# Moving one 4-matmul transpose group behind the weights that were already there

## The chip, the cores and the metric

The kernel runs on one core of a Trainium2 chip. The metric is the device time of one execution in microseconds (us), lower is better. Each comparison is between runs on the same chip; between chips the kernel before moves by a few tenths of a microsecond.

## The reference, cut to what matters

```python
kv  = einsum('bhsd,bhse->bhde', k, v)            # linear attention, batch 8, 8 heads, 576 rows, 64 wide
out = einsum('bhsd,bhde->bhse', q, kv)
out = out / sqrt(mean(out*out, -1) + 1e-6) * g_norm
x   = out as [8, 576, 512]
xn  = (x - mean) / sqrt(var + 1e-6) * g_ln
y   = x + maximum(xn @ w1, 0) @ w2               # w1 is 512 x 2048, w2 is 2048 x 512
```

The rows are cut into 36 tiles of 128. Four tiles come from batch 0's first 512 rows; each needs one "slot" of q. w1 and w2 are loaded in four quarters each.

## The kernel before: the parts that matter

All loads of q, k, v and the weights are issued by GpSimd into one queue, in the order of these lines (each load casts float32 to bfloat16; an extract):

```python
    pool_load(("q", 0, 1), load_slot(qp[0], q, 0, 1), rate1)
    load_w(0, 1)
    pool_load(("q", 0, 2), load_slot(qp[0], q, 0, 2), rate1)
    load_w(1, 1)                                            # w1, second quarter
    load_w(2, 1)                                            # w1, third quarter
    pool_load(("q", 0, 3), load_slot(qp[0], q, 0, 3), rate1)  # last q slot
    load_w(3, 1)                                            # w1, fourth quarter
    ...   # w2's first quarter, batch 1's k and v, w2's second quarter, batch 1's q, the rest of w2
```

A q slot is turned by four TensorE transposes into PSUM, and one copy (by ScalarE or VectorE) takes the result to SBUF. Then four "out" matmuls use it:

```python
    def add_q_turn_pe(b, t, deps, key, eng, h0=0, h1=H):
        ...
        s = add("PE", 0.24 * w, 0.24 * w + 0.26, key, [ident] + list(deps), ..., alloc=("mm", "kvt")[b])
        ...
        e = add(eng, occ, dur, key, [s], lambda: q_turn_out(...))
        s.frees = e
```

The first layer for the first eight tiles works in groups of 16 matmuls, one tile by one quarter of w1 (`m1_fine`):

```python
            g = add("PE", 0.89, 1.1, i, done[a]["xT"] + load["w", 1, c], lambda: m1_fine(a, c), alloc="mm", main=True)
```

Nothing runs in the order of these lines. Each `add` makes a step with a key, and a planner (`run_plan`), with its own estimates of durations, picks the order of every engine before the program is built. On the chip each engine keeps that order. So a changed key can move other steps too, and the order of the built program has to be looked at.

## Time and profile before

| | before |
|---|---|
| time, median of the first three runs | 293.84 us (293.79 to 294.05) |
| profiled span | 292.0 us |
| TensorE busy | 283.9 us, 97% |
| VectorE / ScalarE / GpSimd busy | 57% / 49% / 22% |

### The profile page before, as it was taken

To read this page: it belongs to the slowest core of one execution; us is meant where nothing else is said; L and a number is where in the kernel's file an instruction comes from. 1 tells how busy PE (TensorE), PEld (TensorE's weight loads), DVE (VectorE), ACT (ScalarE), POOL (GpSimd) and SP (SyncE) were. 2 spreads that over 40 slices of the span, in tenths; PEclk is the share of its full clock that TensorE was granted. 3 is DMA by queue.
4 is the path that set the end of the run, shared out by engine and by line. 5 is a ranking of instruction groups with operands and counts; after the bars stand their busy time and mean duration, and the time that the engine had idled before them with its cause. 6 is when DMAs were issued, how large, how long until landed. Compare 5 with 4: busy or idle time off the path is not lost.

```text
span 292.0 us, 5183 instructions
## 1 busy us (share of the span) xinstructions
PE 283.9 (97%) x2057; PEld 161.1 (55%) x2057; DVE 165.2 (57%) x361; ACT 142.6 (49%) x288; POOL 65.6 (22%) x93
## 2 busy tenths in 40 slices
PE   8879999999999999999999999999999999999995
PEld 6668955977745445444544445444544444444444
DVE  2695049578974997557655775477557755320022
ACT  2377964787856612761276127612761177017400
POOL 8974220006407205404050406000000000000000
PEclk9999999999999999999999999999999999999999
DMA  6999999965999997994999399912201310120012
GB/s 98 185 199 205 203 199 170 250 77 76 177 201 111 164 153 161 171 178 105 203 91 174 81 188 119 187 55 90 56 18 54 92 54 18 56 90 18 0 74 73
DMA packets 108716, 35.60 MB, mean 122 GB/s; under 512 B 87187, under 2 KB 104467, under 8 KB 108692
## 3 DMA queue, kind: packets, MB, share of 16 engines
q0 software_dynamic: 72624, 18.35, 65.8%
q1 hardware_dynamic: 35828, 16.79, 26.8%
q8 instruction: 16, 0.26, 0.4%
q10 hardware_dynamic: 240, 0.13, 0.2%
q14 instruction: 8, 0.07, 0.1%
HBM read 36.70 MB, written 9.44 MB: 158 GB/s over the span
## 4 chain that ended last, share of the span: by engine, by line
PE 91%; DMA 4%; POOL 3%; issue 0%; DVE 0%; POOLq 0%
PE mm_ps L643 43%; PE mm_ps L624 33%; PE mm_ps L609 9%; DMA qp<-in_q_dram 4%; PE out_ps L478 3%; PE kv_ps L455 3%; POOL qp L267 1%; PE xT_ps L559 1%; POOL w L348 1%; POOL vb L246 1%; POOL kb L246 1%; PE qT_ps L414 0%; POOL identity masks.py:197 0%; DVE x L650 0%; POOL identity masks.py:199 0%
## 5 line engine op out<-in xcount | busy, mean ns | idle before, releaser
L643 PE MATMUL mm_ps<-w,m 128*128 128x512 bf16 (+2 forms) x608 | 129.5, 368 | 0.0
L624 PE MATMUL mm_ps<-xT,w 128*128 128x512 bf16 x448 | 100.6, 379 | 0.0
L631 ACT ACTIVATE m<-mm_ps 128x512 bf16<-128x512 f32 x112 | 66.8, 597 | 51.4 <-PE mm_ps L624 50.6
L643 PEld LDWEIGHTS <-m 128*128 128x128 bf16 x608 | 57.3, 98 | 60.8
L624 PEld LDWEIGHTS <-w 128*128 128x128 bf16 x448 | 43.1, 98 | 48.9
L500 DVE TENSOR_REDUCE ss<-sq 128x8 f32<-128x512 f32 (+1 forms) x37 | 24.8, 669 | 48.4 <-ACT sq L491 48.4
L650 DVE SCALAR_TENSOR_TENSOR x<-mm_ps,rstd,x 128x512 f32<-128x512 f32 (+2 forms) x38 | 27.2, 719 | 41.7 <-PE mm_ps L643 41.7
L491 ACT ACTIVATE sq<-out_ps 128x512 f32<-128x512 f32 (+1 forms) x37 | 21.5, 584 | 44.4 <-PE out_ps L478 44.4
L609 PE MATMUL mm_ps<-xT,w 128*128 128x128 bf16 x512 | 30.6, 219 | 0.1
L609 PEld LDWEIGHTS <-w 128*128 128x128 bf16 x512 | 29.2, 98 | 1.2 <-issue 0.2
L552 DVE SCALAR_TENSOR_TENSOR xc<-x,mv,gl 128x512 bf16<-128x512 f32 (+1 forms) x38 | 27.2, 723 | 1.1
L495 DVE TENSOR_TENSOR xg<-out_ps,gn 128x512 f32<-128x512 f32 (+1 forms) x37 | 24.7, 668 | 0.2
L616 ACT ACTIVATE m<-mm_ps 128x512 bf16<-128x512 f32 x32 | 18.7, 598 | 5.7 <-PE mm_ps L609 5.5
L728 POOL COPY mark<-xT 128x1 bf16<-128x1 bf16 x15 | 6.5, 435 | 57.4 <-DMA xT<-xc 53.4
L530 DVE TENSOR_TENSOR x<-xg,inv 128x512 f32<-128x512 f32 x24 | 16.6, 692 | 0.8
L504 ACT ACTIVATE rms<-ss,eps_attn 128x8 f32<-128x8 f32 (+1 forms) x37 | 11.1, 300 | 12.1 <-DVE ss L500 11.9
L546 DVE BATCH_NORM_STATS2 stats<-x 128x6 f32<-128x512 f32 x24 | 16.6, 690 | 0.5
L478 PEld LDWEIGHTS <-qT 128*128 128x128 bf16 x160 | 11.3, 98 | 7.1 <-ACT qT L394 1.0
L478 PE MATMUL out_ps<-kv_pack,qT 128*128 128x128 bf16 x160 | 14.5, 219 | 0.6 <-ACT qT L394 0.6
L466 DVE CAST kv_pack<-kv_ps 64x256 bf16<-64x256 f32 x14 | 5.9, 422 | 12.9 <-PE kv_ps L455 12.8
L455 PEld LDWEIGHTS <-kp 128*128 128x128 bf16 (+1 forms) x168 | 10.4, 99 | 2.6 <-DVE kp L396 0.5
L274 POOL DMA_DIRECT2D qp<-in_q_dram x5 | 11.4, 2287 | 0.9 <-issue 0.9
(64 smaller groups left out, 177.3 us busy)
## 6 DMA issues: line engine op xcount, KB each, us to landing
out_dram<-x SPq DMA_DIRECT2D x30, 256.0 KB, 3.2
w<-in_moe_w_ch_dram POOLq DMA_DIRECT2D x8, 512.0 KB, 12.4
vb<-in_v_dram POOLq DMA_DIRECT2D x6, 512.0 KB, 11.6
kp<-in_k_dram POOLq DMA_DIRECT2D x5, 512.0 KB, 8.7
qp<-in_q_dram POOLq DMA_DIRECT2D x5, 512.0 KB, 10.3
out_dram<-x SPq DMA_DIRECT2D x10, 128.0 KB, 3.0
qb<-in_q_dram POOLq DMA_DIRECT2D x2, 512.0 KB, 18.0
qp<-in_q_dram POOLq DMA_DIRECT2D x10, 64.0 KB, 9.9
```

The lines of the kernel that those rows point to most:

```text
L455: nc.tensor.matmul(ps[:, hp, :], lhsT=kp[b % 2][p, t, 2 * hp:2 * hp + 2, :].rearrange("p h d -> p (h d)"), rhs=(v5[b % 2][:, 2 * hp:2 * hp ...
L478: nc.tensor.matmul(o3[:, hp, :], lhsT=att[b]["qT"][:, 4 * t + hp, :], rhs=kv_pack[b % 3][:, hp, :], start=(i == 0), stop=(i == len(bs) - 1))
L491: nc.scalar.activation(sq[:, h0:h1, :], st[n]["ps", h0][:, h0:h1, :], func=AF.Square)
L495: nc.vector.tensor_mul(xg[:, h0:h1, :], st[n]["ps", h0][:, h0:h1, :], gn.to_broadcast([128, h1 - h0, D]))
L500: nc.vector.tensor_reduce(ss[:, h0:h1, :], st[n]["sq"][:, h0:h1, :], axis=AX.X, op=ALU.add)
L552: nc.vector.scalar_tensor_tensor(xc[:, f0:f1], in0=st[n]["x"][:, f0:f1], scalar=blk[m]["mv"][:, i, 0:1], in1=gl[:, f0:f1], op0=ALU.subtrac ...
L609: nc.tensor.matmul(ps[:, d, :], lhsT=w1[c][:, kk, d * 128:(d + 1) * 128], rhs=blk[m]["xT"][:, kk, i * 128:(i + 1) * 128], start=(kk == 0), ...
L616: nc.scalar.activation(st[n]["m1"][:, c, :, :], st[n]["m1ps", c], func=AF.Relu)
L624: nc.tensor.matmul(ps, lhsT=w1[c][:, kk, d * 128:(d + 1) * 128], rhs=blk[m]["xT"][:, kk, :], start=(kk == 0), stop=(kk == nKm - 1))
L631: nc.scalar.activation(blk[m]["m1", c][:, d, :], blk[m]["m1ps", g], func=AF.Relu)
L643: nc.tensor.matmul(st[n]["m2ps", f0], lhsT=m1_piece(n, c, d), rhs=w2[c][:, d, f0:f1], start=(c == 0 and d == 0), stop=(c == 3 and d == 3))
L650: nc.vector.scalar_tensor_tensor(x[:, f0:f1], in0=st[n]["m2ps", f0], scalar=blk[m]["rstd"][:, i, :], in1=x[:, f0:f1], op0=ALU.mult, op1=AL ...
```

## The change

Its intent: TensorE stands still for 0.5 us at the turn of batch 0's last q slot, whose load has not landed, while the third quarter of w1, which it needs next, has. Put the turn behind the first group on that quarter, and let ScalarE do its copy.

```diff
     for t in (1, 2, 3):
-        q_turned = add_q_turn_pe(0, t, load["q", 0, t], (-4.5, pos[1] - 3.7, -3.2)[t - 1],
-                                 ("ACT", "ACT", "DVE")[t - 1])
+        q_turned = add_q_turn_pe(0, t, load["q", 0, t], (-4.5, pos[1] - 3.7, 2.1)[t - 1],
+                                 ("ACT", "ACT", "ACT")[t - 1])
```

## The prediction

> **What bounds the kernel now.** I read the page's first two parts, then the chain that ended last, then the start of that chain in order of time, and then TensorE (PE), the weight loads and GpSimd around the one wait that the change aims at.
>
> The first line of part 1 and the first two lines of the chain part of the page:
>
> ```profile
> PE 283.9 (97%) x2057; PEld 161.1 (55%) x2057; DVE 165.2 (57%) x361; ACT 142.6 (49%) x288; POOL 65.6 (22%) x93
> ...
> PE 91%; DMA 4%; POOL 3%; issue 0%; DVE 0%; POOLq 0%
> ```
>
> TensorE is the bound: busy 283.9 of 292.0 us, 91% of the chain. No other engine is above 57%. The only other thing of size in the chain is "DMA 4%". The chain in order of time, 20 to 27 us, shows what that is:
>
> ```profile
> 11.06 11.47 DMA qp<-in_q_dram
> 22.53 0.05 issue
> 22.57 0.40 PE qT_ps L414 x4
> 22.97 0.89 PE mm_ps L609 x16
> ```
>
> The load of batch 0's last q slot (issued at 11.06) lands at 22.53, and the four transposes that turn it start at 22.57. Everything after hangs on them: from there the chain is TensorE alone, except one "issue" piece of 0.01 us, until the end. So one microsecond won at 22.57 would be one microsecond of the run, if nothing else takes its place. The TensorE timeline on both sides:
>
> ```profile
> 19.22 2.85 PE L609 MATMUL mm_ps<-xT,w 128*128 128x128 bf16 x48
> 22.57 0.40 PE L414 MATMUL qT_ps<-identity,qp 128*128 128x128 bf16 x4 [0.50 <-DMA qp<-in_q_dram]
> 22.81 1.06 PE L609 MATMUL mm_ps<-xT,w 128*128 128x128 bf16 x16
> 23.70 0.39 PE L478 MATMUL out_ps<-kv_pack,qT 128*128 128x128 bf16 x4
> 23.92 0.39 PE L559 MATMUL xT_ps<-identity,xc 128*128 128x128 bf16 x4
> ```
>
> The bracket is the wait: 0.50 us after the modelled end of the last matmul. Counted by starts it is more: the last matmul before it starts at 21.855 and the pitch of these matmuls is 0.0558 us (219 ns each, pipelined), so the transposes could have started at 21.91; 22.573 - 21.911 = 0.66 us. **0.66 us is the most that this change can win.**
>
> The weight loads three microseconds later, which stand in no list of waits, matter most. Two answers of the weight-load timeline, one that ends and one that begins at 25.095:
>
> ```profile
> 24.65 0.38 PEld L609 LDWEIGHTS <-w 128*128 128x128 bf16 x6
> ...
> 25.10 0.56 PEld L609 LDWEIGHTS <-w 128*128 128x128 bf16 x10
> ```
>
> The reader is to see a hole: the first stretch ends at 25.03, the next starts at 25.10. 25.10 is where the first tile meets w1's fourth quarter. Matmul starts there are 24.985 and 25.103, a step of 0.118 where the pitch is 0.056: a hidden wait of 0.06 us. The DMA semaphore in the trace says for what: the fourth quarter's last increment is at 25.06. GpSimd shows the same landing, a little later, because its next load reuses that semaphore:
>
> ```profile
> 21.97 1.58 POOL L350 DMA_DIRECT2D w<-in_moe_w_ch_dram  x2 [1.62 <-DMA w<-in_moe_w_ch_dram]
> 25.34 0.69 POOL L261 DMA_DIRECT2D qp<-in_q_dram  x1 [1.79 <-DMA w<-in_moe_w_ch_dram]
> ```
>
> Semaphore records of the loads concerned: second quarter 19.17, third quarter 21.69 (GpSimd goes on at 21.97), last q slot 22.53, fourth quarter 25.06 (GpSimd goes on at 25.34). TensorE is thus already at the pace of the loads at 25.10, with 0.06 us to spare the other way.
>
> **What the Trainium skill says.** (1) "TensorE: Matmul & The Clock Gate", Part 2, "Step-by-step": only weight loads are pulled ahead; matmuls keep program order. So transposes that wait for q hold back matmuls whose data is there. The trace agrees: the third quarter landed at 21.69 and was first used at 22.81. (2) "DMA: Bandwidth & Descriptors", "Two DMAs through the same engine are not ordered": in one queue of a DMA engine descriptors start in order. So the fourth quarter, issued behind the q slot, lands when the queue gets there, whoever reads it. The trace agrees: landings are in the order of issue, 2.53 us apart. (3) Same page, "Why a DMA increments its semaphore by 16 and not by 1": only the full 16 mean that all data landed. For the fourth quarter 15 increments are in at 24.09 and the last at 25.06. (4) "Perfetto Trace Analysis", "Optimizing Scalar/DVE Operations": a PSUM access costs ScalarE about 51 ns fixed, VectorE about 125. That alone would favour ScalarE; in this trace the same 128x512 bf16 copy takes 0.42 us on VectorE and 0.58 on ScalarE, and these are used below.
>
> **The change part by part.** I compared the instruction order of both programs. The arithmetic is the same; what moves is:
>
> 1. *Transposes.* Before: transposes of q (4), third quarter on tile 0 (16), out of tile 3 (4), turn of tile 2 (4), third quarter on tile 1 (16), fourth quarter. After: 16, transposes of q (4), turn of tile 2 (4), 16, out of tile 3 (4), fourth quarter. The same 44 matmuls stand between the second quarter and the fourth. The third quarter landed at 21.69, before 21.91, so the wait at 22.57 is gone. The q transposes come at 21.91 + 16 x 0.0558 = 22.80, after the landing at 22.53: no wait either.
>
> 2. *Where TensorE then arrives.* 21.91 + 44 x 0.0558 = 24.37 is when the fourth quarter's first matmul could start, where before it was 22.573 + 44 x 0.0558 = 25.03, and in fact 25.10. But the data is complete at 25.06. So TensorE waits 25.10 - 24.37 = **0.73 us there, in place of 0.66 + 0.06 = 0.72 us in two places. Sum: 0.**
>
> 3. *The copy on ScalarE.* +0.58 busy there, -0.42 on VectorE. ScalarE is free for it: the eviction before it starts at about 23.0 (0.49 pitch), the copy runs from about 23.5 to 24.1; its reader, out of tile 3, is due at 24.15. Even a late copy has the 0.7 us of idle TensorE behind it. Worth 0.
>
> 4. *Tile 3's later steps.* Its square starts about 0.25 us later (out of tile 3 at 24.15 and not 23.70), so its xc is done at about 28.4 and not 28.12. Its turn moves behind the third quarter on tile 2: 25.10 + 5 x 0.893 = 29.57. No wait. From the last of these transposes to the first matmul that needs them there is one group of 16: 0.95 us. The path through ScalarE needs, from the same point in the old kernel, 0.25 to the start of its copy, 0.59 for the copy and 0.05 for the wake-up: 0.89. It fits by about 0.06 us; that is the tightest new place, worth 0 to 0.05.
>
> 5. *Batch 1's k copies on ScalarE* slip by about 0.07 us; the kv matmuls need the second one 12 matmuls (0.67 us) after their start, and in the old trace it was done at 35.20 against a need at 35.8. Worth 0.
>
> GpSimd's list is the same, and SyncE's is in the stretch compared (names without buffer numbers). From 34.3 us on TensorE runs the same list. Sum: 0, with -0.05 to +0.05 either way.
>
> **The rivals.** *Full gain:* 0.66 us, 293.2 us. For it: the chain names the q load and nothing else, and TensorE follows without a listed wait. Against it: the 0.06 us hole at 25.10 and the landing at 25.06. It would need the fourth quarter to land 0.7 us sooner, and the loads are issued the same. *A partial gain:* landings jitter from run to run. The old start at 25.10 is the later of two landings that differ by only 0.06 us in effect; where q is the late one, the change wins the difference. I estimate 0 to 0.1 us. *A loss:* the new tight place (4), or ScalarE behind with an eviction so that TensorE lacks a PSUM buffer. ScalarE is busy 8.41 of 9.20 us between 25.1 and 34.3, so a delay isn't quickly made up there. For a loss of 0.2 us it would have to run late by more than any step above shows. *Clock:* one idle stretch of 0.73 us in place of 0.66; the old trace keeps PE clock 1.00 through the 0.66, and the skill ("TensorE: Matmul & The Clock Gate", Part 1) puts re-throttling at idle windows of about 3.4 us. I give it nothing.
>
> **Range and chances.** 293.84 plus 0, less 0.03 for the jitter case: 293.8 us. The old kernel's own runs span 293.79 to 294.05, so the range must hold that and a small gain or loss: 293.5 to 294.1. Full gain (293.2) lies outside on purpose; I give it one chance in twelve. Two per cent is 5.9 us, and all idle TensorE time after 19 us is about 1.1 us: within 2% is nearly sure.
>
> **What would show it.** Right: no wait at the q transposes, third-quarter matmuls from about 21.91, a wait of about 0.7 us on the w load ahead of the weight loads at about 25.10, and no other new gap. The chain should name the w load where it named q. Wrong: fourth-quarter matmuls at about 24.4 (full gain), or a gap ahead of the matmuls at about 30.7 (tile 3's turn) or of an eviction's successor (loss). The prediction is wrong if the fourth quarter's landing moves from 25.06.

## More of the kernel before

TensorE is the bound for most of the span. For much of the first fifth of it the DMA engines are nearly full as well. Part 2 of the page has one digit per 7.3 us, the busy tenths of TensorE and of the DMA engines:

```profile
PE   8879999999999999999999999999999999999995
...
DMA  6999999965999997994999399912201310120012
```

A 9 means 90% or more. The reader is to see that from 22 to 58 us both rows are at 9 (the DMA row already from 7 us): TensorE works, and the DMA engines are hardly ever idle.

## The result, and the profile after

| | before | after |
|---|---|---|
| median of four runs each | 293.94 us (293.79 to 294.14) | 293.69 us (293.62 to 293.99) |
| ratio, 95% interval | | 0.9993 (0.9976 to 1.001) |
| profiled span | 292.0 us | 291.9 us |

A ratio is the mean time of one kernel's fast runs over that of the other's of the same rounds, so it is not quite the ratio of the medians. The interval holds 1: no difference is shown.

The busy times and the chain of the changed kernel, from its page:

```profile
PE 283.2 (97%) x2029; PEld 162.1 (56%) x2057; DVE 164.8 (56%) x360; ACT 143.3 (49%) x289; POOL 65.6 (22%) x93
...
PE 88%; DMA 4%; POOL 4%; DVE 2%; issue 1%; POOLq 0%
```

One copy has gone from VectorE (x361 to x360) to ScalarE (x288 to x289). The matmul count is 28 lower only because some matmul records are missing from this trace; the weight loads, 2057 in both, are all there, and I count by them below. The chain still holds 4% DMA. Which load it is has changed; the chain in order of time, 10 to 30 us (start, length, what):

```profile
12.05 12.78 DMA w<-in_moe_w_ch_dram
24.83 0.05 issue
24.88 4.64 PE mm_ps L609 x80
```

Before, the chain ran back from TensorE to the q slot at 22.53. Now it runs back to the fourth quarter of w1 at 24.83. The TensorE timeline of the changed kernel:

```profile
19.51 3.74 PE L609 MATMUL mm_ps<-xT,w 128*128 128x128 bf16 x64
23.08 0.39 PE L414 MATMUL qT_ps<-identity,qp 128*128 128x128 bf16 x4
23.31 0.39 PE L559 MATMUL xT_ps<-identity,xc 128*128 128x128 bf16 x4
23.53 1.06 PE L609 MATMUL mm_ps<-xT,w 128*128 128x128 bf16 x16
24.42 0.39 PE L478 MATMUL out_ps<-kv_pack,qT 128*128 128x128 bf16 x4
24.88 4.64 PE L609 MATMUL mm_ps<-xT,w 128*128 128x128 bf16 x80
```

The 64 matmuls of the first line are three groups on the first two quarters and the first group on the third, without a break: the wait for q is gone. The turn at 23.08 has no bracket either. A break is left ahead of the last line. TensorE could have gone on at 24.65 and went on at 24.88. The list of waits of the weight loads (who waited for whom, total us, times, longest), first of the kernel before, 20 to 61 us, then of the changed one, 19.8 to 62 us:

```profile
PEld L414 <- DMA qp<-in_q_dram: 0.7, 1, 0.7
PEld L478 <- DMA qT<-qp: 0.2, 1, 0.2
```

```profile
PEld L609 <- DMA w<-in_moe_w_ch_dram: 0.2, 1, 0.2
PEld L478 <- ACT qT L394: 0.2, 1, 0.2
```

The wait for q has turned into a wait for w1, and a second new one has come: "out" (L478) waits for a copy of ScalarE. That one is at 41.55 us, for batch 1's q, and I had not foreseen it. By starts it is 0.20 us, and the turn just before it (40.03 us) waits 0.10 more, too short for the list. The experiments are about these two.

### The profile page after: what moved, and what is told of

The parts are those of the page before. It is cut to its first block, busy times and chain, and to the rows that moved or that the text cites. A ratio compares the mean times of both kernels' runs of the same rounds, so it can differ in the third digit from the quotient of the medians.

```text
span 291.9 us, 5154 instructions
## 1 busy us (share of the span) xinstructions
PE 283.2 (97%) x2029; PEld 162.1 (56%) x2057; DVE 164.8 (56%) x360; ACT 143.3 (49%) x289; POOL 65.6 (22%) x93
## 4 chain that ended last, share of the span: by engine, by line
PE 88%; DMA 4%; POOL 4%; DVE 2%; issue 1%; POOLq 0%
PE mm_ps L643 41%; PE mm_ps L624 32%; PE mm_ps L609 8%; DMA w<-in_moe_w_ch_dram 4%; PE out_ps L478 3%; PE kv_ps L455 3%; POOL qp L267 1%; POOL w L348 1%; POOL vb L246 1%; PE xT_ps L559 1%; DVE x L650 1%; POOL kb L246 1%; PE qT_ps L414 0%; DVE stats L546 0%; DVE x L530 0%
## 5 line engine op out<-in xcount | busy, mean ns | idle before, releaser
L643 PE MATMUL mm_ps<-w,m 128*128 128x512 bf16 (+2 forms) x592 | 128.1, 367 | 0.7
L624 PE MATMUL mm_ps<-xT,w 128*128 128x512 bf16 x436 | 99.6, 379 | 0.5
L504 ACT ACTIVATE rms<-ss,eps_attn 128x8 f32<-128x8 f32 (+1 forms) x37 | 11.1, 300 | 12.2 <-DVE ss L500 12.1
L478 PE MATMUL out_ps<-kv_pack,qT 128*128 128x128 bf16 x160 | 14.5, 219 | 0.9 <-ACT qT L394 0.6
L478 PEld LDWEIGHTS <-qT 128*128 128x128 bf16 x160 | 11.2, 98 | 7.1 <-ACT qT L394 1.2
L455 PE MATMUL kv_ps<-vb,kp 128*128 128x128 bf16 (+1 forms) x144 | 11.3, 227 | 0.3 <-DMA vb<-in_v_dram 0.3
```

Of the source, the lines that this page charges most:

```text
L455: nc.tensor.matmul(ps[:, hp, :], lhsT=kp[b % 2][p, t, 2 * hp:2 * hp + 2, :].rearrange("p h d -> p (h d)"), rhs=(v5[b % 2][:, 2 * hp:2 * hp ...
L478: nc.tensor.matmul(o3[:, hp, :], lhsT=att[b]["qT"][:, 4 * t + hp, :], rhs=kv_pack[b % 3][:, hp, :], start=(i == 0), stop=(i == len(bs) - 1))
L624: nc.tensor.matmul(ps, lhsT=w1[c][:, kk, d * 128:(d + 1) * 128], rhs=blk[m]["xT"][:, kk, :], start=(kk == 0), stop=(kk == nKm - 1))
L643: nc.tensor.matmul(st[n]["m2ps", f0], lhsT=m1_piece(n, c, d), rhs=w2[c][:, d, f0:f1], start=(c == 0 and d == 0), stop=(c == 3 and d == 3))
```

## The experiments

The DMA semaphores in the trace tell when each load landed: a load adds 16, and I take the time of the last. From the profiled run of each kernel (us; the columns two to four and six are landings):

| kernel | second quarter | last q slot | fourth quarter | fourth less q | batch 1's q | load 521 less batch 1's q | waits |
|---|---|---|---|---|---|---|---|
| before | 19.17 | 22.53 | 25.06 | 2.53 | 38.69 | 11.10 | 0.75 |
| after | 19.19 | 22.30 | 24.83 | 2.53 | 38.82 | 11.07 | 0.61 |
| e1 | 19.71 | 23.06 | 25.58 | 2.52 | 39.18 | 11.14 | 0.74 |
| e2 | 18.64 | 21.93 | 24.49 | 2.56 | 38.92 | 11.94 | 1.81 |
| e3 | 18.84 | 22.21 | 24.72 | 2.51 | 38.35 | 11.08 | 0.72 |
| e4 | 19.52 | 22.87 | 25.39 | 2.52 | 38.99 | 11.08 | 0.68 |
| e5 new | 19.55 | none | 24.58 | | 38.12 | 11.30 | 0.00 |
| e5 old | 19.42 | none | 24.51 | | 38.05 | 12.22 | 0.04 |
| e6 | 18.72 | 21.91 | 25.30 | 3.39 | 39.15 | 11.08 | 1.38 |
| e10 | 19.34 | 22.69 | 25.21 | 2.52 | 38.81 | 10.40 | 0.00 |
| e11 | 19.57 | 22.87 | 25.39 | 2.52 | 38.98 | 11.15 | 0.50 |

"Load 521" is the 521st weight load, near 50 us: all kernels have done the same work by then. "Waits" is the time from the first weight load on the second quarter to load 521, less the 29.83 us that it takes in e5 new and e10, where TensorE waits for nothing in between.

My theory: one queue of loads sets TensorE's pace from 19 to 42 us, and several loads are needed just when they land; taking away the wait for one of them brings the wait for the next. Rivals: the copy on ScalarE takes back what the move wins; another engine binds after 25 us; the wait for q was the only one and its 0.66 us should reach the end.

### e1: only the copy moves to ScalarE

```diff
 kernel before
-                                 ("ACT", "ACT", "DVE")[t - 1])
+                                 ("ACT", "ACT", "ACT")[t - 1])
```

> The old place of the last q slot's turn, its copy on ScalarE (half of the change). My theory (the loads of w1 set the pace): the wait of 0.5 us at the q transposes stays, the first fourth-quarter matmuls start at the landing of that quarter or 2.5 us after the q slot's, about 25.1 us, as in the kernel before; time the same within 0.2 us. Rival (the copy on ScalarE delays its evictions and costs something that the move wins back): slower than the kernel before by 0.3 us or more, with a new wait of TensorE on ScalarE after 25 us.

Measured: 293.85 us against 293.74, ratio 1.0002 (0.9989 to 1.0014). Correct. The weight loads from 20 to 62 us wait only here:

```profile
PEld L414 <- DMA qp<-in_q_dram: 0.7, 1, 0.7
```

So the copy on ScalarE costs nothing that shows by itself, and no wait on ScalarE follows. The rival with the copy falls.

### e2: only the turn moves, its copy stays on VectorE

```diff
 changed kernel
-                                 ("ACT", "ACT", "ACT")[t - 1])
+                                 ("ACT", "ACT", "DVE")[t - 1])
```

> The new place of the turn, its copy left on VectorE (the other half). The planner then also puts tile 2's first group (first quarter of w1, 0.89 us) ahead of the fourth quarter, so TensorE has work until 24.37 + 0.89 = 25.26, past the landing at about 25.06. My theory: no wait at the q slot nor at the fourth quarter; TensorE is 0.5 to 0.7 us ahead of the kernel before at 30 us, and then stopped by the next load, batch 1's q, which lands at 38.8 and needs ScalarE until 41.5; so 0 to 0.3 us faster in the end. Rival (no later load is near): the whole 0.66 us reaches the end, about 293.2 us. Rival (the move itself is worth nothing): TensorE no sooner at 30 us.

Measured: 294.59 us against 293.74, ratio 1.0028 (1.0016 to 1.0041). Correct, and slower by 0.8 us, which none of my theories had. The TensorE timeline shows both halves of what happened:

```profile
24.41 5.52 PE L609 MATMUL mm_ps<-xT,w 128*128 128x128 bf16 x96
29.77 0.39 PE L559 MATMUL xT_ps<-identity,xc 128*128 128x128 bf16 x4
30.83 1.33 PE L609 MATMUL mm_ps<-xT,w 128*128 128x128 bf16 x21 [0.67 <-ACT xT L566]
...
39.61 0.92 PE L414 MATMUL qT_ps<-identity,qp 128*128 128x128 bf16 x8 [0.25 <-ACT qp L394]
```

With the copy on VectorE the planner put tile 2's first group ahead of the fourth quarter, and there was no wait at 25 us at all, as expected: 96 matmuls from 24.41 on. But it also put tile 3's turn (29.77) behind tile 2's last group, directly ahead of the group that needs it, and TensorE waited for ScalarE's copy, 0.84 us by starts. And at 39.6 it reached batch 1's q with one group of the second layer fewer behind it than in the kernel before, and waited again. Load 521 came 11.94 us after batch 1's q, not 11.1: that one group, 0.86 us, was still to be done. With this planner the move alone is not to be had by the key: other steps go with it.

### e3 and e4: both orders, with nothing to wait for at the fourth quarter

```diff
 kernel before (e3) / changed kernel (e4); tile 0 wrong on purpose
-                    ps[:, d, :], lhsT=w1[c][:, kk, ...],
+                    ps[:, d, :], lhsT=w1[2 if (n, c) == (0, 3) else c][:, kk, ...],
```

> The kernel before, but tile 0's fourth-quarter group reads the third quarter's weights (tile 0 wrong on purpose), so that no load is waited for there; same order of instructions. My theory: the 0.06 us hole at 25.1 goes, the 0.5 us wait for q stays; group starts at about 25.03; same time within 0.2 us as the kernel before. Control for the next run.

> The changed kernel with the same edit (tile 0 wrong on purpose). My theory: the fourth quarter's landing is what swallows the gain; without that wait TensorE starts the group at about 24.4, 0.6 us ahead of the control, and no wait is left between 22 and 30 us. It then meets batch 1's q (out of tiles 4 and 5 at about 41.5) and loses most of the lead there: 0 to 0.3 us faster than the kernel before in the end. Rival (the q wait was worth nothing, or ScalarE holds TensorE back): the group starts no sooner than 25.0. Rival (full gain): 0.6 us ahead also after 42 us and at the end.

Measured: e3 293.81 us, ratio 0.9999 (0.9986 to 1.0012); e4 293.94 us, ratio 1.0004 (0.999 to 1.0017). Both wrong in tile 0. e3 waits for q as before, with one 0.7 us wait of the weight loads. e4's order wins at the first place what the prediction called the most that can be won: its first group of tile 0 on the fourth quarter's place starts 1.79 us after the q slot's landing (24.66 less 22.87), that of e3 2.46 us after (24.67 less 22.21). A lead of 0.67 us. Then e4's list of waits of the weight loads, 19.8 to 43 us:

```profile
PEld L414 <- ACT qp L394: 0.8, 2, 0.5
PEld L478 <- ACT qT L394: 0.2, 1, 0.2
```

Both are at 39.7 to 41.7 us. ScalarE rearranges batch 1's q (four copies from its landing on), TensorE turns two slots of it, and ScalarE copies the second turn. By starts the three gaps are 0.16, 0.28 and 0.20 us, 0.64 in all. The whole lead is gone: load 521 comes 11.08 us after batch 1's q in both. This settles two things. The fourth quarter's landing is what takes the gain in the changed kernel, and with it out of the way batch 1's q takes it.

### e5: the last q slot is not loaded

```diff
 changed kernel / kernel before; the turn reads slot 2, wrong on purpose
-    pool_load(("q", 0, 3), load_slot(qp[0], q, 0, 3), rate1)
+    pool_load(("q", 0, 3), (lambda: None, 128 * H * 256), rate1)   # planned, not issued
-                qp[b % 2][:, t, ...], identity)
+                qp[b % 2][:, 2 if (b, t) == (0, 3) else t, ...], identity)
```

> The changed kernel without the load of the last q slot (its turn reads slot 2, a wrong result on purpose); all instructions of the other engines in the same order. Theory (the loading queue sets TensorE's pace from 19 to 42 us): the fourth quarter lands some 0.84 us after the third less, so all later loads are 0.8 us sooner; no wait at the fourth quarter (TensorE arrives at 24.4, data at about 24.2), none at batch 1's q; 0.6 to 0.8 us faster at the end, about 293.1 us. Rival (TensorE, ScalarE or VectorE bind after 25 us and the loads do not): within 0.2 us of the changed kernel.

> The same edit on the kernel before: the turn stands at its old place and has nothing to wait for. Theory: as fast as the last run within 0.2 us, 0.6 to 0.8 us faster than the kernel before: once the queue is shorter the place of the turn makes no difference. Rival (the old place of the turn costs something of its own, beside the wait for its data): slower than the last run by 0.3 us or more.

Measured: new 293.59 us, ratio 0.9992 (0.9979 to 1.0005); old 293.55 us, ratio 0.9996 (0.9981 to 1.001). Both wrong. In the traces the theory holds: the fourth quarter lands 2.50 and 2.53 us after the third, where it was 3.36 and 3.37 with the q slot between them, so the slot costs 0.85 us of the queue; and no weight load waits between 20.5 and 62 us in either. The two orders are alike once the queue is shorter. But I expected 0.6 to 0.8 us at the end, and the means are only 0.1 to 0.2 us lower, with 0 inside the intervals. By time alone the first run's rival (within 0.2 us of the changed kernel) fits as well; only the traces speak for the theory. The profiles suggest why the times do not. TensorE's first work on the second quarter came at 19.59 and 20.40 us in these two, at 19.22 and 19.45 in the kernels before and after: executions differ in how late they are before this stretch begins. In the second of the two the early loads were late already (slot 1 of q landed at 13.48 us, in the kernel before at 12.20). Where TensorE waits for loads later on, such lateness can hide in the wait; where it doesn't, it stays. From that first work to the last weight load it was 268.27 and 268.17 us here, 269.05 before and 268.73 after, 0.5 to 0.9 us less. That lateness explains the missing half microsecond is read from two profiles and not tested.

### e6: one more load in the queue

```diff
 changed kernel
+    nc.gpsimd.dma_start(spare, q[0, :, 0:512, :]...[:, 3, :, :])   # issued just ahead of load_w(3, 1); nobody reads spare
```

> The changed kernel with one more load of the same kind and size (a q slot into a tile that nobody reads), issued between the last q slot and the fourth quarter; right result, all other engines in the same order. Theory: fourth quarter and all that follow land about 0.84 us later, TensorE waits that much longer at the fourth quarter (about 1.5 us in all) and the run is 0.7 to 0.9 us slower, about 294.6 us. Rival (loads are hidden there): the same within 0.2 us.

Measured: 294.94 us against 293.76, ratio 1.0041 (1.0028 to 1.0054), so about 1.2 us slower. Correct.

```profile
23.98 0.39 PE L485 MATMUL out_ps<-kv_pack,qT 128*128 128x128 bf16 x4
25.35 0.84 PE L616 MATMUL mm_ps<-xT,w 128*128 128x128 bf16 x12 [0.98 <-DMA w<-in_moe_w_ch_dram]
```

The fourth quarter lands 3.39 us after the q slot in place of 2.53, 0.86 later, and the wait there is 1.14 us by starts. A load that nobody needs is paid in full, and somewhat more than the 0.7 to 0.9 that I expected; the rest I have not traced. In the trace, of the fastest of the five executions, the waits up to load 521 are 0.77 us more than in the changed kernel (1.38 against 0.61). Loads are not hidden in this stretch.

### e7: a try at a faster load order

```diff
 changed kernel (the edit in short)
-    load_w(3, 1)
+    # the fourth quarter in two loads, columns 0 to 255 and 256 to 511
-        load_w(1, 2); batch 1's q
+        batch 1's q; load_w(1, 2)
```

> A try at a version that beats both: the changed kernel with the fourth quarter of w1 loaded in two halves (each output half of the first group waits for its own) and batch 1's q loaded ahead of w2's second quarter; the planner moves batch 1's turn forward with it. Theory: first half lands at about 24.0, before TensorE arrives at 24.4, so the wait at the fourth quarter shrinks from up to 0.73 to about 0.25 us; batch 1's q lands near 36.5, so nothing stops TensorE at 41 us; 0.2 to 0.5 us faster. Rival (every load of this stretch is needed by the time it lands, so that a swap only moves the wait on): a new wait of TensorE on w2's second quarter at about 39 us and no gain.

Measured: 295.38 us against 293.76, ratio 1.0056 (1.0042 to 1.007). Correct, and 1.6 us slower. The first half landed at 24.11 and TensorE did not wait for it (24.64); the second landed at 25.50:

```profile
24.64 0.61 PE L611 MATMUL mm_ps<-xT,w 128*128 128x128 bf16 x8
25.55 0.62 PE L611 MATMUL mm_ps<-xT,w 128*128 128x128 bf16 x8 [0.30 <-DMA w<-in_moe_w_ch_dram]
```

So the split only moved the wait to the second half, 0.47 us by starts where I had expected 0.25. A larger loss came later: batch 1's turn moved forward, with it the DMA transposes of its other slots (39.34 in place of 40.91 us), and the load of batch 2's q landed at 61.15 in place of 58.51. At 69.2 us "out" waited for batch 2's turn, 0.8 us by starts. That was neither my theory's gain nor its rival's wait at 39 us.

### e8 and e9: both orders, freed of both loads

```diff
 e4 (e8) / e3 (e9): batch 1's q is still loaded, but ScalarE's copies read batch 0's
-             qb[:, :, t0:t1, :]...
+             qp[0][:, t0:t1, :, :] if b == 1 else qb[:, :, t0:t1, :]...
```

> The changed kernel freed of both later waits: tile 0's fourth-quarter group reads the third quarter (as in e4), and ScalarE's copies of batch 1's q read batch 0's q, which is there already (results wrong on purpose; all loads still run, in the same order). Theory (the wait for q moves from load to load; take the next two away and the gain stays): no wait on w1 at 25 us, none on ScalarE at 39 to 42 us; the lead of about 0.65 us over the next run's order lasts to the end, 0.4 to 0.7 us faster than e9 and than the kernel before. Rival (the lead is lost to something else than these two loads): no faster than e9 by more than 0.2 us, with another new wait.

> The same two edits on the kernel before: control. Theory: the wait at q, 0.66 us by starts, stays and sets all that follows; 0 to 0.2 us faster than the kernel before, since only small slacks behind it are gone. Rival: as fast as e8.

Measured: e8 295.49 us, ratio 1.0048 (1.0025 to 1.007); e9 294.59 us, ratio 1.003 (1.0016 to 1.0044). Both are slower than the kernel before, and e8's median lies above e9's, though their intervals overlap: the times refute what I expected. Up to 60 us the traces are as the theory has them: in e8 no weight load waits between 19.8 and 60 us; e9 waits for q at 22.4 and has 0.51 us more of waits by load 521. What follows spoils the comparison, here e8 on TensorE:

```profile
60.92 0.56 PE L478 MATMUL out_ps<-kv_pack,qT 128*128 128x128 bf16 x7 [0.41 <-DMA qT<-qp]
...
69.12 0.62 PE L478 MATMUL out_ps<-kv_pack,qT 128*128 128x128 bf16 x8 [0.39 <-DMA qT<-qp]
```

As in e7, the DMA transposes of batch 1 went out sooner (40.21 and 40.28 us), batch 2's q landed later (61.24 and 62.27), and "out" waited at 61 and 69 us. So the pair says nothing on whether the lead would have reached the end. Why earlier transposes go with later loads is open; three kernels show the two together, and I tested no cause. Earlier transposes are not the only way to it: in e6 they went out at 41.38 us, no earlier than before, and batch 2's q landed at 60.49, 2.0 us later than before; the added load itself takes 0.86 us of the queue.

### e10: refilling TensorE at both places

```diff
 changed kernel
-                                 ("ACT", "ACT", "ACT")[t - 1])
+                                 ("ACT", "ACT", "DVE")[t - 1])
+    ...   # lines that collect the steps named below are left out
+    mains_made[3].behind = mains_made[7].behind = mains_made[8]   # tile 2's first group ahead of the two fourth-quarter groups
+    mains_made[11].behind = done[3]["turn"]                       # tile 3's turn ahead of tile 2's last group
+    for s in q1_turns:                                            # batch 1's two turns on TensorE
+        s.behind = mains_made[21]                                 # behind one more group of the second layer
```

> A right version that should beat both: the new place of the turn, its copy on VectorE; tile 2's first group put ahead of the two fourth-quarter groups (0.89 us of work while that load lands), tile 3's turn kept ahead of tile 2's last group (in e2 it came behind it and TensorE waited 0.84 us), and batch 1's turn put one group of the second layer later than in the changed kernel (two later than in e2), so that TensorE has 0.86 us more to do before it needs batch 1's q. Theory: no wait at q, at the fourth quarter, at 30 us or at 40 us above 0.1 us each; 0.4 to 0.7 us faster than the kernel before, about 293.2 us. Rival (w2's third quarter, landing at 41.2, or another load is next in line): a new wait on a load between 38 and 47 us and less than 0.2 us gained.

Measured: 293.25 us against 293.75, ratio 0.9979 (0.9966 to 0.9992). Correct, and the only kernel whose interval lies below 1: about 0.6 us by the ratio, 0.5 by the medians, as expected. The TensorE timeline, 19 to 31 us:

```profile
19.38 3.75 PE L610 MATMUL mm_ps<-xT,w 128*128 128x128 bf16 x64
22.96 0.39 PE L414 MATMUL qT_ps<-identity,qp 128*128 128x128 bf16 x4
...
24.53 4.63 PE L610 MATMUL mm_ps<-xT,w 128*128 128x128 bf16 x80
28.99 0.39 PE L560 MATMUL xT_ps<-identity,xc 128*128 128x128 bf16 x4
```

From 19.4 us on there is no wait at q, at the fourth quarter (landed at 25.21, first used at 25.4), at tile 3's turn or at batch 1's q. Load 521 comes 10.40 us after batch 1's q: this order is no longer held by it. The first wait is 0.2 us at 60.3, for a DMA transpose that the kernel before waits for too. I did not run the same refill with the turn at its old place, so what the move itself gives to the 0.6 us is not shown.

### e11: batch 1's turn later, and nothing else

```diff
 changed kernel (the line that collects q1_turns is left out)
+    for s in q1_turns:
+        s.behind = mains_made[21]
```

> One part of e10 alone: the changed kernel with batch 1's turn one group of the second layer later (0.86 us more work before TensorE needs batch 1's q), the fourth quarter's wait left as it is. Theory: the wait at the fourth quarter stays (0.2 to 0.7 us by starts), none at batch 1's q; since those two loads are tied within about 0.3 us, 0 to 0.3 us faster than the kernel before, less than the 0.5 us of e10. Rival (batch 1's q alone is the bound and the fourth quarter is of no account): as fast as e10, about 0.5 us faster than the kernel before.

Measured: 293.98 us against 294.16, ratio 0.9995 (0.9975 to 1.0014). Correct. The wait on the w load stays:

```profile
PEld L610 <- DMA w<-in_moe_w_ch_dram: 0.5, 1, 0.5
```

and none on batch 1's q is left. The trace has 0.50 us of waits in the stretch, where e10 has none. The intervals of e10 and e11 overlap, so it is the traces and not the times that tell them apart: taking away either wait alone (e4, e11) leaves half a microsecond or more of waits; e10, which covers both with work, has none.

## Why the prediction was right

**The sum of 0 was right, and so was its reason.** The wait for q went, the turn at its new place waits for nothing, and the fourth quarter's landing took over. The table says why this was no accident of one run: in every run of it that has both loads back to back the fourth quarter lands 2.51 to 2.56 us after the q slot, and TensorE's 44 matmuls between the two take 2.46. An old order that waits for the q slot is then back at the fourth quarter within about 0.1 us of that landing, so an order that merely swaps the work ahead of it has no more than that to win there. In the changed kernel's own run the old order would have gone on at 22.30 + 0.04 + 2.46 = 24.80, by the same steps as in the prediction, and the data was there at 24.83.

The time by itself does not confirm this reason, and there is some luck in how well the number was met: e4, which is free of the wait for the fourth quarter, is as slow as the kernel before, because of a second load that the prediction did not have (below). What confirms the reason is the wait on w1 in the trace, and e4's start of that group 0.67 us sooner than e3's.

**The terms were mis-sized.** The prediction had "0.73 us there, in place of 0.66 + 0.06". Measured at the fourth quarter was 0.23 us (24.65 to 24.88). TensorE was 0.28 us later there than foreseen from the trace that I had (24.65 against 24.37), of which 0.23 us was there at its first work on the second quarter (19.45 against 19.22), and the load was 0.23 us sooner. I had put the landings' jitter into a gain of 0 to 0.1 us. It is larger, over 1 us from run to run for one load (24.49 to 25.58 without the edits of e5 and e6). It did no harm because the two landings move together. By its letter one of my signs of being wrong came true, "if the fourth quarter's landing moves from 25.06": it moved to 24.83. But the q slot's moved with it, from 22.53 to 22.30, and the distance stayed 2.53 us. The distance is what the sign should have named.

**ScalarE's part was right.** The copy ran from 23.78 for 0.58 us, and "out" started at 24.42 without a wait; e1 shows it costs nothing alone. Tile 3's turn came at 29.36, ScalarE's copy of it at 29.78, and no wait followed. Two lines of ScalarE's timeline:

```profile
23.78 0.58 ACT L394 COPY qT<-qT_ps 128x512 bf16<-128x512 bf16 x1
...
29.78 0.59 ACT L566 COPY xT<-xT_ps 128x512 bf16<-128x512 bf16 x1 [0.34 <-PE xT_ps L559]
```

**One wait was not foreseen.** I argued against the full gain only with the fourth quarter, and wrote that it "would need the fourth quarter to land 0.7 us sooner". e4 shows that this would not be enough: batch 1's q, a load that TensorE needs 17 us later by way of ScalarE, stood ready to take the same 0.66 us. In the changed kernel itself it took 0.30 us (0.10 and 0.20 by starts), against the sign "no other new gap". It showed nowhere in the list of waits before, since TensorE arrived as late as its data. By e4, even one chance in twelve for the full gain was too much.

**The clock** was granted at 0.999 to 1.0 in all four runs of the changed kernel; I had given it nothing, and that was right.

## What to carry to other kernels

When a tuned kernel shows one wait on a load, compare the landing times of the following loads of that queue with the times at which they are first used: if the next ones are used the moment they land, removing the listed wait only moves it. Work that is ready has to be put in front of every such load, or the queue has to be made shorter; an order that only swapped work ahead of the same load won nothing here. And when a planner decides the order, look at everything that a changed key moves: here the choice of engine for one copy moved three other groups and cost 0.8 us.

## What the Trainium skill lacked or had wrong

- "DMA: Bandwidth & Descriptors", "Why a DMA increments its semaphore by 16 and not by 1", says that only the full 16 count, not how far apart they can be. In seven runs (before, after, e1 to e4 and e10) the first increment for the fourth quarter came at 23.12 to 23.35 us, within 0.23 us, and the last at 24.49 to 25.58. In the kernel before, the 15th was in at 24.09 and the 16th at 25.06. In the seven runs the last increment came 0.14 us (e2) to 0.99 us (e1) after the 15th, and the 15th itself moved by 1.08 us from run to run (23.95 in e3 to 25.03 in e4): the last few increments set the landing and its jitter.
- The same page's "Anatomy of one DMA" gives a fit for one load. No page gives the rate of casting loads (float32 read, bfloat16 written) that queue behind each other. Here a q slot (262,144 bytes read in pieces of 256) took 0.85 us of the queue, 308 GB/s, and a quarter of w1 (1,048,576 bytes) 2.53 us, 414 GB/s, both by the distance of landings.
- "Perfetto Trace Analysis", "Optimizing Scalar/DVE Operations", gives fixed costs of a PSUM access that, taken alone, favour ScalarE. For a 128x512 bf16 copy out of PSUM the whole instruction was shorter on VectorE: it took 0.58 us on ScalarE and 0.42 us on VectorE.
- No page tells by how much DMA transposes and loads beside them hold each other up. In e7, e8 and e9 the transposes went out 0.6 to 1.6 us sooner than in the kernel before and the next batch's q landed 2.6 to 3.8 us later; the cause is not known, and in e6 that load was 2.0 us late without it.
